# Own PSUM tiles for the experts' first products, expert operands on one base modulo 256 bytes, and a new priority table

## The chip, the core and the metric

The kernel runs on one core of a Trainium2 chip. The metric is device time in microseconds (us) of one execution; three runs of the kernel before are shown with their median. Five engines work side by side, each on its own instruction queue: PE (TensorE, matmuls), DVE (VectorE), ACT (ScalarE), POOL (GpSimd) and SP (which only issues DMAs here). An instruction waits at the head of its queue until what it needs is there; what stands behind it on that engine waits with it.

## The reference

Attention with 4 sink keys and a window of 128 keys (batch 4, 8 heads, 768 positions, head size 64), then a mixture of 8 experts with the two best experts per token (3072 tokens, 512 features, 1024 hidden):

```python
scores = np.where(is_sink | in_window, scale * q @ k.T, -1e9)
a = softmax(scores); x = (a @ v) as [3072, 512]
noisy = x @ w_gate + log1p(exp(x @ w_noise)) * noise
top2 = the two largest of noisy per token, their weights a softmax over the two
for e in range(8):
    h = np.maximum(x[rows of e] @ w1[e], 0.0)
    out[rows of e] += weight * (h @ w2[e])
```

## The kernel before, in words

Every piece of work is recorded as an operation with an engine, a modelled duration and a priority (`Plan.op`); `Plan.run` then simulates the engines and emits the instructions of each engine in the order that this list schedule gives. The priorities of the attention and routing operations come out of one table of numbers, `PR`. There are two plans, emitted one behind the other: `phase_one` (attention, routing of the first three batches, the first rows and weights of expert 0) and `phase_two` (routing of the last batch, all experts).

Attention runs over 48 steps (16 pairs of heads, 3 blocks of 256 queries): scores on PE (L315, into the PSUM tile `S`), softmax on DVE, ACT and POOL (`mn`, `cbuf`, `sm`), transposes of the weights (L380) and of the sink part (L397, from `pcbuf`), products with the values (L406, L409, L418), rows out. Each batch ends with its logits (L601, transposed back by L609) and its routing: ranks by matmul (L714 to L720), the place of each token in its expert's list (L806, `idg`). With the places known, an indirect DMA gathers rows (L891, later L897), DVE scales them (L942), they are transposed (PE, L952, for expert 0; DVE, L957, for the others) and split into a high part `skn` (ACT, L966) and a rest `sqn` (DVE, L215).

Each expert's rows are cut into two pieces of at most 512 rows. For each piece, the hidden features go in 8 blocks of 128. A block has an "up" (`up_block`): 12 matmuls of the piece's width, L1048 to L1050, that sum w1 times rows into one PSUM half `H`; then ACT writes the relu's high part (`up_h`, L1097), DVE the rest (`up_l`, L1105), both into `h`; and later a "down" (`down`, L1116 to L1118, L1121 and L1122 for the last tile) multiplies `h` with w2 (two tiles, `w2a` and `w2b`) into the PSUM banks `Y`. PE runs the up of a block while the rests of an earlier block are made, then the downs of that earlier block. In the last piece all eight ups come first and then all downs (`apart`). The finished rows are scaled (L1125) and added to the output by an indirect DMA (L1140).

`H` and `X` (PSUM for transposes and routing of the second phase) are not tiles of their own: they are the two halves of one `S` tile each, handed out by `plan.views`:

```python
pair = plan.get("S", room(sh) + 1, [128, 2, 512], F32, "wide")
plan.views["X"] = lambda i: pair[:, i % 2]
plan.views["H"] = lambda i: plan.get("S", room(sh))[:, i % 2]
```

Waits between engines are set per tile. Thus the relu of a block (ACT) also waits for the rest of the block before it (DVE), because both halves count as one tile: of the 128 relu instructions L1097, 90 carry a wait on DVE. `up_ahead` records the first two ups of expert 0 (24 matmuls) already in `phase_one`, so they stand between the last logits.

Of the kernel before, what the change touches and what calls it, by code (L numbers as in the profile page):

```python
# [20 lines left out]
PR = dict(cur=-8431.651, cur1=-7439.283, cur1_0=218.223, cur1_9=-1416.941, cur_0=0.0, cur_9=-191.213, dv=-2620.133,  # L21
          dv_0=-188.761, dv_9=-58.0, exps=-79.031, exps_0=-733.766, exps_9=-686.771, ga=0.0, gt=185.39, lg=-1781.795,
          load_qk=4173.715, load_v=245.644, mins=-994.502, mins_0=35.968, mins_9=5432.878, nosink=-4343.446,
          nosink_0=462.054, nosink_9=43.061, pcopy=-1854.216, pcopy_0=972.034, pcopy_9=77.513, plow=-3587.377,
          plow_0=-204.859, plow_9=-701.943, prev=-1305.7, prev_0=-151.842, prev_9=314.934, ptr=-349.555,
          ptr_0=-1749.435, ptr_9=-10.037, ptr_c=-3954.256, ptr_c_0=-264.44, ptr_c_9=56.179, ptr_m=-1635.596,
          ptr_m_0=182.224, ptr_m_9=-0.973, pv=-632.746, pv_0=479.582, pv_9=-76.04, pv_c=-4613.603, pv_c_0=-4.393,
          pv_c_9=16.777, qk=-1178.393, qk_0=631.58, qk_9=-3710.152, rows_c=12808.825, rows_c_0=-665.082,
          rows_c_9=-7472.954, rt=-15225.06, sink_c=-3756.417, sink_c_0=0.0, sink_c_9=16.368, sinks=-2.103,
          sinks_0=1336.99, sinks_9=-790.624, sub=-299.026, sub_0=1233.464, sub_9=50.854, sums=0.0, sums_0=723.554,  # L30
          sums_9=-13.305, sums_i=-3243.012, sums_i_0=-939.503, sums_i_9=-291.364, w1=4288.053, pctr_0=777.383,
          pctr=0.0, pctr_9=57.978, ga_l=-998.334, gt_l=111.981, ll=0.0, ua=22395.225, dv_pool=1, sm_act=10, cm_pool=9,
          pc_pool=0, gap_8=2, et=42, gap=1, stay=2496.59)
# [3 lines left out]
COLD = 5.0  # L37
SLACK = .008
WARM = 32
FIRST = 4  # L40
AHEAD = 2
# [7 lines left out]
class Plan:  # L49
# [5 lines left out]
    def __init__(self, nc, pools, rings, cold=0.0):  # L55
        self.nc = nc
        self.pools = pools
        self.rings = dict(rings)
        self.cold = cold
        self.live = {}  # L60
        self.views = {}
        self.shapes = {}
        self.count = {}
        self.ops = []
        self.touch = {}
        self.wrote = {}

    def get(self, tag, i, shape=None, dt=F32, pool="sb", pad=None):
        kx = (tag, i)
        if tag in self.views:  # L70
            x = self.views[tag](i)
            if shape is None:
                shape = self.shapes[kx]
            else:
                self.shapes[kx] = shape = (shape, pad)
            shape, pad = shape
            to = pad or shape
            x = x[:, :math.prod(to[1:])]
            if len(to) == 3:
                x = x.rearrange("p (a b) -> p a b", a=to[1])  # L80
            return x if to == shape else x[tuple(slice(0, n) for n in shape)]
# [163 lines left out]
def attention(tc, plan, cst, sh, kqs, v, vss, xbuf):  # L245
# [17 lines left out]

    def warm():
# [44 lines left out]
    def qk(n, a):  # L309
        g, j, _ = at(n, 2 * a)  # L310
        for h in range(2):
            r = slice(h * D, (h + 1) * D)
            p = get("S", 2 * n + a, [128, 2, 512], F32, "wide")[:, h, :2 * KW].rearrange("p (a b) -> p a b", a=2)
# [570 lines left out]
def gather(plan, nc, cst, sh, xbuf, e, t, z, after=None):  # L884
# [5 lines left out]
    def go():  # L890
        nc.gpsimd.indirect_dma_start(  # L891
            out=plan.get("xg", n, [128, sh.XW], F32, "early"), out_offset=None, in_=xbuf[:128 + (b + 1) * sh.S],
            in_offset=bass.IndirectOffsetOnAxis(ap=cst["idg"][:, t:t + 1], axis=0))

    def part(i):
        x = plan.get("xg", n, [128, sh.XW], F32, "early").rearrange("p (i d) -> p i d", d=sh.SW)
# [31 lines left out]
def rows_turn(plan, nc, cst, sh, e, t, size, ring, z):  # L928
# [15 lines left out]
    def spot():  # L944
        if ring == "S":
            return get(ring, ti, [128, 2, 512], F32, "wide")[:, 0, :].rearrange("p (c s) -> p c s", c=c)
# [92 lines left out]
def room(sh):  # L1039

    return sh.B * (sh.H // 2) * (sh.S // 128) + 1


# [7 lines left out]


def up_ahead(plan, nc, cst, sh, f, z):

    width = 128 * FIRST

    def go(i):
        up_block(plan, nc, sh, plan.get("S", room(sh), [128, 2, 512], F32, "wide")[:, f % 2, :width], 0, f, i, halves(plan, sh, 0), width)

    for i in range(sh.DM // 128):  # L1060
        plan.op("PE", 3 * (width / 2400 + .016), z, lambda i=i: go(i),
                r=[(x, 0, t) for x in ("xh", "xl") for t in range(FIRST)] + [w_tile(plan, 1, 0, f // 2)[0]], w=[("H", f)],
                u=[("S", room(sh))])


def experts(tc, plan, cst, sh, w1, w2, xbuf, out):
# [91 lines left out]
    z = 0  # L1158
# [5 lines left out]
    for q, (e, tiles, width) in enumerate(info):  # L1164
# [130 lines left out]
def phase_one(tc, nc, plan, ac, tail, cst, sh, kq, v, vs, w1, w2, xbuf, out):  # L1295
# [18 lines left out]
    def first_rows(t, ring, zg, zt):  # L1314
        gather(plan, nc, cst, sh, xbuf, 0, t, zg)
        weight(plan, nc, cst, sh, 0, t, zt)
        if ring == "S":
            plan.count["S"] = 2 * NJ * HP * sh.B - 1
# [22 lines left out]
    for f in range(AHEAD):  # L1341
# [113 lines left out]
```

## Time and profile before

| what | value |
|---|---|
| median of 3 runs | 787.09 us (786.73 to 788.6) |
| the profiled execution | 783.96 us, its span 782.3 us |
| clock of TensorE granted, mean | 0.998 of full speed |
| PE busy | 744.1 us, 95% of the span |
| DVE / ACT / POOL busy | 454.7 / 333.4 / 437.6 us |
| attention and three routings, 0 to 192 us | PE 175.6, DVE 172.0, ACT 148.8, POOL 142.5 us busy |
| experts, 270 to 500 us | PE 227.7 of 230 us busy |
| last piece's ups, 738 to 760 us | PE 16.6 of 22 us busy |

Busy time is the union of the instructions' spans on an engine. Matmuls are pipelined: one instruction's span (0.39 us for 512 columns) is longer than the step from its start to the start of the next (0.23 us), so a gap of the engine costs more than the idle time that a row shows in brackets. Until about 192 us DVE is nearly as busy as PE; from there on PE is busy all but a few per cent, and the question of each gap is what ended last before it.

### The profile page before, as it was taken

The page shows a single profiled execution, that of the slowest core. Times are in us where ns is not written, and L with a number is a line of the kernel's source. Part 1 is how long each engine was busy: PE and PEld are TensorE (multiplying, and loading weights), DVE is VectorE, ACT ScalarE, POOL GpSimd, SP SyncE. Part 2 cuts the span into 40 slices and gives each one's busy share as a digit, 9 for nine tenths or more (in the row PEclk, how much of TensorE's full clock was granted, in tenths as well). Part 3 has the DMA queues.
Part 4 walks back from the last instruction along what each step waited for, and adds up shares of the span by engine and source line. Part 5 has one row for each costly group of instructions (what it writes and reads, how often), then busy time and mean ns, then how long its engine had stood idle before and what let it go on. Part 6 is the DMA issues. An engine that isn't in the chain of part 4 may idle for free.

```text
span 782.3 us, 12963 instructions
## 1 busy us (share of the span) xinstructions
PE 744.1 (95%) x4499; PEld 618.9 (79%) x4499; DVE 454.7 (58%) x1181; ACT 333.4 (43%) x927; POOL 437.6 (56%) x625
## 2 busy tenths in 40 slices
PE   9999998789999999999999999999999999999975
PEld 4667676566778898889888987898898889888864
DVE  7889998987754554645364446526544643464210
ACT  6987996784114413341333143323413431451211
POOL 7665878875246375356727462747275473747202
PEclk9999999999999999999999999999999999999999
DMA  6568698565636753553445363517452652544213
GB/s 221 175 169 203 203 261 216 138 162 132 168 96 127 238 110 50 156 138 57 94 127 131 53 134 114 109 40 155 123 101 47 172 134 36 125 133 71 26 16 41
DMA packets 58372, 97.80 MB, mean 125 GB/s; under 512 B 19232, under 2 KB 31776, under 8 KB 58304
## 3 DMA queue, kind: packets, MB, share of 16 engines
q1 hardware_dynamic: 44928, 69.34, 30.5%
q0 software_dynamic: 13376, 27.60, 20.3%
q8 instruction: 36, 0.59, 0.3%
q14 instruction: 32, 0.26, 0.1%
HBM read 68.51 MB, written 28.40 MB: 124 GB/s over the span
## 4 chain that ended last, share of the span: by engine, by line
PE 70%; DVE 9%; issue 7%; ACT 6%; POOL 3%; DMA 3%; POOLq 0%; SPq 0%; DVEq 0%; ACTq 0%
PE S L1048 11%; PE S L1050 10%; PE S L1049 10%; PE Y L1118 9%; PE Y L1116 9%; PE Y L1117 9%; PE S L315 2%; DMA xg<-x_rows,rt_idq 2%; PE X L406 2%; ACT cbuf L346 2%; PE P L380 1%; DVE h L1105 1%; PE X L409 1%; DVE xg L942 1%; POOL out L1140 1%
## 5 line engine op out<-in xcount | busy, mean ns | idle before, releaser
L897 POOL DMA_INDIRECT xg<-x_rows,rt_idq x174 | 176.1, 1012 | 62.2 <-issue 53.3
L1105 DVE SCALAR_TENSOR_TENSOR h<-S,h 128x384 fp32r<-128x384 f32 (+4 forms) x168 | 75.7, 470 | 203.5 <-ACT h L1097 153.2
L1097 ACT ACTIVATE h<-S 128x384 fp32r<-128x384 f32 (+4 forms) x128 | 64.3, 503 | 290.8 <-PE S L1050 210.1
L1048 PE MATMUL S<-skn,w 128*128 128x384 f32 (+4 forms) x512 | 177.7, 347 | 10.0 <-DVE h L1105 10.0
L1050 PE MATMUL S<-skn,w 128*128 128x384 f32 (+4 forms) x512 | 175.9, 344 | 0.0
L1049 PE MATMUL S<-sqn,w 128*128 128x384 f32 (+4 forms) x512 | 175.6, 343 | 0.0
L1140 POOL DMA_INDIRECT out<-y,idx x53 | 91.7, 1730 | 57.5 <-ACT y L1125 40.9
L1149 POOL COPY spacer<-h 1x1 f32<-1x1 f32 x88 | 28.7, 326 | 157.6 <-ACT h L1097 156.8
L1048 PEld LDWEIGHTS S<-skn,w 128*128 128x128 f32 x512 | 96.1, 188 | 22.4 <-DVE h L1105 10.4
L1049 PEld LDWEIGHTS S<-sqn,w 128*128 128x128 f32 x512 | 96.1, 188 | 6.2
L1050 PEld LDWEIGHTS S<-skn,w 128*128 128x128 f32 x512 | 96.0, 188 | 2.5
L1118 PE MATMUL Y<-w2a,h 128*128 128x512 f32 x192 | 76.1, 397 | 2.3 <-DVE h L1105 1.8
L1116 PE MATMUL Y<-w2a,h 128*128 128x512 f32 x192 | 75.7, 394 | 0.7 <-ACT h L1097 0.7
L1116 PE MATMUL Y<-w2b,h 128*128 128x512 f32 x192 | 76.1, 396 | 0.0
L1117 PE MATMUL Y<-w2b,h 128*128 128x512 f32 x192 | 75.8, 395 | 0.0
L1118 PE MATMUL Y<-w2b,h 128*128 128x512 f32 x192 | 75.8, 395 | 0.0
L1117 PE MATMUL Y<-w2a,h 128*128 128x512 f32 x192 | 75.6, 394 | 0.0
L315 PE MATMUL S<-kq 64*128 64x264 f32 (+1 forms) x384 | 56.4, 401 | 4.3 <-DVE cbuf L325 1.6
L215 POOL TENSOR_TENSOR cbuf<-cbuf,mn 128x528 f32<-128x528 f32 x48 | 51.4, 1076 | 13.4 <-DVE mn L335 5.5
L966 ACT ACTIVATE skn<-xtn 128x512 fp32r<-128x512 f32 (+2 forms) x46 | 27.9, 606 | 61.7 <-DVE xtn L957 54.7
L346 ACT ACTIVATE cbuf<-cbuf 128x132 f32<-128x132 f32 x160 | 48.0, 314 | 6.6 <-POOL cbuf L215 6.2
L1118 PEld LDWEIGHTS Y<-w2a,h 128*128 128x128 f32 x192 | 36.1, 188 | 14.0 <-DVE h L1105 4.8
(212 smaller groups left out, 1298.3 us busy)
## 6 DMA issues: line engine op xcount, KB each, us to landing
st<-in_w1l SPq DMA_DIRECT2D x32, 512.0 KB
st<-in_w2l SPq DMA_DIRECT2D x32, 512.0 KB
kq<-in_kq SPq DMA_DIRECT2D x15, 792.0 KB
out<-zt SPq DMA_DIRECT2D x31, 256.0 KB
vn<-in_v SPq DMA_DIRECT2D x16, 384.0 KB
x_rows<-xr SPq DMA_DIRECT2D x48, 128.0 KB
xg<-x_rows,rt_idq POOLq DMA_INDIRECT x174
st<-in_vs SPq DMA_DIRECT2D x4, 256.0 KB
```

Of the source, the lines that this page charges most:

```text
L315: nc.tensor.matmul(p[:, :2 if j else 1], kq(g)[r, j // 2, 2 + j % 2, NS:], x[:, :2 if j else 1], start=True, stop=True)
L346: nc.scalar.activation(C(n)[:, u], C(n)[:, u], AF.Exp, scale=1.0 / math.sqrt(D), accum_out=get("sm", n, [128, 4])[:, u:u + 1])
L897: nc.gpsimd.indirect_dma_start(out=x[:, i, :], out_offset=None, in_=xbuf.rearrange("r (q d) -> (r q) d", d=sh.SW), in_offset=bass.Indirect ...
L1048: nc.tensor.matmul(p, w[:, 0], xh, start=(i == 0), stop=False)
L1049: nc.tensor.matmul(p, w[:, 0], xl, start=False, stop=False)
L1050: nc.tensor.matmul(p, w[:, 1], xh, start=False, stop=(i == sh.DM // 128 - 1))
L1097: nc.scalar.activation(get("h", FC * q + f, [128, 2 * 128 * FIRST], F32R)[:, :width], get("H", FC * q + f, [128, width], F32, "ps", [128, ...
L1105: nc.vector.scalar_tensor_tensor(h[:, o:o + s1 - s0], p[:, s0:s1], 0.0, h[:, s0:s1].bitcast(F32), op0=OP.max, op1=OP.subtract)
L1116: nc.tensor.matmul(p, hh, w[:, 0], start=(f == 0), stop=False)
L1117: nc.tensor.matmul(p, hh, w[:, 1], start=False, stop=False)
L1118: nc.tensor.matmul(p, hl, w[:, 0], start=False, stop=(f == FC - 1))
L1140: d = nc.gpsimd.indirect_dma_start(out=out, out_offset=bass.IndirectOffsetOnAxis(ap=c["idx"][:size(e, t), e, t:t + 1], axis=0), in_=get("y ...
```

## The change

The halves go: `H` gets two PSUM tiles of one bank each and `X` two, all four in the second phase's PSUM pool, and `S` goes back into the first phase's pool. The code for views is removed. With it goes `up_ahead`: the two first ups of expert 0 are now in the second plan like all others, behind the last logits; the relus and rests of expert 0's first piece get a priority 400 earlier. The gathered rows `xg` are padded from 2240 to 2304 bytes and a filler of 64 bytes (`even`) is put into the `tail` pool; with the order in which the tiles are made, this lays w1, w2a, w2b, `skn`, `sqn`, `h` and `xg` all to base 64 modulo 256. Before, these bases were 64 (w1), 0 (`skn`, `sqn`, w2a), 224 (w2b), 192 (`h`) and 64, 0, 192, 128, 64 (the five `xg`). The whole table `PR` is replaced; of its choices, `pc_pool` 0 to 2 moves 12 of the 48 copies into `pcbuf` from ACT to POOL. The instructions of each engine are otherwise the same in number.

```diff
-PR = dict(cur=-8431.651, cur1=-7439.283, cur1_0=218.223, cur1_9=-1416.941, cur_0=0.0, cur_9=-191.213, dv=-2620.133,
...
-          pc_pool=0, gap_8=2, et=42, gap=1, stay=2496.59)
+PR = dict(cur=-10653.273, cur1=-2090.412, cur1_0=-442.426, cur1_9=73.44, cur_0=-4.596, cur_9=0.0, dv=0.64,
...
+          ga_l=-1277.079, gt_l=1521.637, ll=320.211, ua=-4.272, sm_act=10, dv_pool=1, cm_pool=9, pc_pool=2, gap=2,
+          gap_8=3, et=36, stay=1992.355)
...
+LINE = 64
-AHEAD = 2
...
     def get(self, tag, i, shape=None, dt=F32, pool="sb", pad=None):
         kx = (tag, i)
-        if tag in self.views:
-            x = self.views[tag](i)
...
+    for i in range(2):
+        get("S", i, [128, 2, 512], F32, "ps")
...
-            out=plan.get("xg", n, [128, sh.XW], F32, "early"), out_offset=None, in_=xbuf[:128 + (b + 1) * sh.S],
+            out=plan.get("xg", n, [128, sh.XW], F32, "early", [128, LINE * -(-sh.XW // LINE)]), out_offset=None, in_=xbuf[:128 + (b + 1) * sh.S],
...
-def up_ahead(plan, nc, cst, sh, f, z):
...
-            if k >= AHEAD:
-                op("PE", UP1 * width + .19, zu, lambda q=q, f=f: up(q, f),
-                   r=[(x, e, t) for x in ("xh", "xl") for t in tiles] + [w_tile(plan, 1, e, f // 2)[0]], w=[("H", k)],
-                   u=[(nm, NP + q) for nm in ("skn", "sqn")])
-            op("ACT", .06 + width / 1200, zu, lambda q=q, f=f: up_h(q, f), r=[("H", k)], w=[("hh", k)], u=[("h", k)])
-            op("DVE", .08 + width / 950, zu, lambda q=q, f=f: up_l(q, f), r=[("H", k), ("hh", k)], w=[("hl", k)], u=[("h", k)])
+            op("PE", UP1 * width + .19, zu, lambda q=q, f=f: up(q, f),
+               r=[(x, e, t) for x in ("xh", "xl") for t in tiles] + [w_tile(plan, 1, e, f // 2)[0]], w=[("H", k)],
+               u=[(nm, NP + q) for nm in ("skn", "sqn")])
+            zh = zu if q else zu - 400
+            op("ACT", .06 + width / 1200, zh, lambda q=q, f=f: up_h(q, f), r=[("H", k)], w=[("hh", k)], u=[("h", k)])
+            op("DVE", .08 + width / 950, zh, lambda q=q, f=f: up_l(q, f), r=[("H", k), ("hh", k)], w=[("hl", k)], u=[("h", k)])
...
-    for f in range(AHEAD):
-        up_ahead(plan, nc, cst, sh, f, PR.get("ua", 60) + f)
...
-    plan.rings.update(y=4, h=9, X=2)
-    plan.count["X"] = 1
-    pair = plan.get("S", room(sh) + 1, [128, 2, 512], F32, "wide")
-    plan.views["X"] = lambda i: pair[:, i % 2]
-    plan.views["H"] = lambda i: plan.get("S", room(sh))[:, i % 2]
+    plan.rings.update(y=4, h=9, X=2, H=2, w2b=2)
+    for i in range(2):
+        plan.get("H", i, [128, 128 * FIRST], F32, "ps", [128, 512])
+    plan.get("X", 0, [128, NT + 1, sh.E], F32, "ps", [128, 64, 8])
+    plan.get("h", 0, [128, 2 * 128 * FIRST], F32R)
+    plan.get("w2b", 0, [128, 2, 1024], F32R)
...
+            tail.tile([128, 16], F32, name="even")
```

From the first down of the experts on, the instructions of every engine stand in the same order as before. What changes there is which waits they carry. On ACT, in the last piece, the relu's line is L1097 before and L1068 after; y is the scaled result. Before:

```order
L1097 ACTIVATE h<-S 128x384 [waits DVE_49,PE_49]
L1097 ACTIVATE h<-S 128x384 [waits DVE_49,PE_49,Pool_49]
L1125 ACTIVATE y<-Y,wc_77 128x512 [waits DMASW7_49,PE_49]
L1097 ACTIVATE h<-S 128x384 [waits DVE_49,Pool_49]
L1125 ACTIVATE y<-Y,wc_77 128x512 [waits DMASW1_49,PE_49,Activation_49]
L1125 ACTIVATE y<-Y,wc_77 128x512 [waits DMASW2_49,PE_49,Activation_49]
L1097 ACTIVATE h<-S 128x384 [waits PE_49,Pool_49] x4
```

And on ACT after, in the same place:

```order
L1068 ACTIVATE h<-H 128x384 [waits PE_49,Activation_49] x2
L1068 ACTIVATE h<-H 128x384 [waits PE_49,Pool_49]
L1096 ACTIVATE y<-Y,wc_77 128x512 [waits DMASW7_49,PE_49]
L1068 ACTIVATE h<-H 128x384 [waits PE_49,Pool_49]
L1096 ACTIVATE y<-Y,wc_77 128x512 [waits DMASW1_49,PE_49,Activation_49]
L1096 ACTIVATE y<-Y,wc_77 128x512 [waits DMASW2_49,PE_49,Activation_49]
L1068 ACTIVATE h<-H 128x384 [waits PE_49,Pool_49] x4
```

No row moved; the waits of the relus on DVE are gone (of the 128 relus 90 carried one, now 2). On PE, an up waits for the rest (DVE) of the block two before it, which used its bank; before, it waited for the rest of the block right before it.

On PE at the end of the first phase (L952 and L941 are the transposes of the last tile of expert 0's first rows, whose rows are gathered with the places of the third batch; X<-xtn,wbd are logits; X<-idf,lt turns them back). Before:

```order
L418 MATMUL X<-ps,vr 128x128
L609 MATMUL X<-idf,lt 128x128 x2
L1048 MATMUL S<-skn,w_1580 128x512
L1049 MATMUL S<-sqn,w_1580 128x512 [waits DVE_49]
L1050 MATMUL S<-skn,w_1580 128x512
L601 MATMUL X<-xtn,wbd 32x256 [waits Activation_49]
L601 MATMUL X<-xtn,wbd 32x256 x3
L609 MATMUL X<-idf,lt 128x128 [waits Activation_49]
L609 MATMUL X<-idf,lt 128x128
L1048 MATMUL S<-skn,w_1580 128x512
```

And on PE after:

```order
L590 MATMUL X<-xtn,wbd 32x256 [waits Activation_49]
L941 MATMUL S<-idf,xg 128x128 [waits DMASW3_49,DVE_49]
L941 MATMUL S<-idf,xg 128x128 x3
L598 MATMUL X<-idf,lt 128x128 [waits Activation_49]
L598 MATMUL X<-idf,lt 128x128
L598 MATMUL X<-idf,lt 128x128 [waits Activation_49]
L598 MATMUL X<-idf,lt 128x128
L1032 MATMUL H<-skn,w_1607 128x512 [waits DVE_49,PE_49]
L1033 MATMUL H<-sqn,w_1607 128x512
```

The transposes of the last tile stood ahead of the last two attention steps' products with the values (L406); they moved to right behind the last logits. The first up stood between the logits; it now stands behind all of them and behind those transposes. The placing of the third batch (L806, now L795) moved too: six of the 48 products with the values stood behind it before, three stand behind it now.

## Rows read from the trace of the kernel before

**Rows 1.** The page, part 1: busy us, share of the span, instructions of each engine

```profile
PE 744.1 (95%) x4499; PEld 618.9 (79%) x4499; DVE 454.7 (58%) x1181; ACT 333.4 (43%) x927; POOL 437.6 (56%) x625
```

**Rows 2.** Busy in the first stretch: PE, PEld, DVE, ACT, POOL, clock, DMA, GB/s

```profile
0.00:192.00 192.00, 175.60 (x1694) 121.20 (x1694) 172.01 (x507) 148.84 (x636) 142.45 (x247) 1.00 0.68 188
```

**Rows 3.** Waits of PE, whole run: us in total, times, longest us

```profile
PE S L1048 <- DVE h L1105: 10.0, 10, 1.6
...
PE Y L1118 <- DVE h L1105: 1.8, 6, 0.5
```

**Rows 4.** The same view, from 240 us on (its L1048 row is unchanged)

```profile
PE Y L1118 <- DVE h L1105: 1.3, 5, 0.3
PE Y L1118 <- DVE gw L1031: 0.5, 2, 0.3
```

**Rows 5.** Timeline of PE, last piece: start, duration, [idle before <- what ended it]

```profile
743.08 0.34 PE L1050 MATMUL S<-skn,w 128*128 128x384 f32 x1
744.64 0.44 PE L1048 MATMUL S<-skn,w 128*128 128x384 f32 x1 [1.23 <-DVE h L1105]
744.92 0.34 PE L1049 MATMUL S<-sqn,w 128*128 128x384 f32 x1
...
746.67 0.34 PE L1050 MATMUL S<-skn,w 128*128 128x384 f32 x1
```

**Rows 6.** Timeline of ACT and DVE in the same place

```profile
743.51 0.49 ACT L1097 ACTIVATE h<-S 128x384 fp32r<-128x384 f32 x1 [4.02 <-PE S L1050]
...
744.03 0.56 DVE L1105 SCALAR_TENSOR_TENSOR h<-S,h 128x384 fp32r<-128x384 f32 x1 [5.11 <-ACT h L1097]
```

**Rows 7.** Timeline of DVE and PE around 350 us

```profile
350.15 0.56 DVE L1105 SCALAR_TENSOR_TENSOR h<-S,h 128x384 fp32r<-128x384 f32 x1 [1.99 <-PE S L1050]
...
350.77 0.50 PE L1118 MATMUL Y<-w2a,h 128*128 128x512 f32 x1 [0.26 <-DVE h L1105]
351.10 0.39 PE L1116 MATMUL Y<-w2a,h 128*128 128x512 f32 x1
```

**Rows 8.** Timeline of DVE around 260 us, behind a gather

```profile
260.34 0.16 DVE L1031 TENSOR_TENSOR gw<-xg,perm 32x8 f32<-32x8 f32 x1 [2.93 <-DMA xg<-x_rows,rt_idq]
...
261.97 0.52 DVE L1105 SCALAR_TENSOR_TENSOR h<-S,h 128x256 fp32r<-128x256 f32 x2
```

**Rows 9.** Timeline of PE: first and last of 9, then of 11 downs

```profile
301.93 0.40 PE L1116 MATMUL Y<-w2b,h 128*128 128x512 f32 x1
...
303.80 0.39 PE L1118 MATMUL Y<-w2b,h 128*128 128x512 f32 x1
...
306.45 0.39 PE L1116 MATMUL Y<-w2a,h 128*128 128x512 f32 x1
...
308.74 0.39 PE L1118 MATMUL Y<-w2a,h 128*128 128x512 f32 x1
```

**Rows 10.** Timeline of PE around 165 us: operands on unequal, then on equal bases

```profile
165.04 0.66 PE L380 MATMUL P<-idf,cbuf 128*128 128x128 f32 x4
165.46 0.64 PE L418 MATMUL X<-ps,vr 128*128 128x128 f32 x4
```

**Rows 11.** Timeline of PE, POOL and DVE: from the placing to the first downs

```profile
168.40 0.54 PE L806 MATMUL X<-rt_tc,rt_op 128*128 128x56 f16 x12
...
171.76 1.09 POOL L891 DMA_INDIRECT xg<-x_rows,idg  x1 [0.17 <-issue]
172.87 0.26 POOL L215 TENSOR_TENSOR pcbuf<-cbuf,pcbuf 128x32 fp32r<-128x32 f32 x1
...
177.93 0.90 DVE L942 TENSOR_TENSOR xg<-xg 128x512 f32<-128x512 f32 x1
...
182.30 0.68 DVE L215 TENSOR_TENSOR sqn<-S,skn 128x512 fp32r<-128x512 f32 x1
...
188.19 0.38 PE L609 MATMUL X<-idf,lt 128*128 128x128 f32 x2
...
194.08 0.50 PE L1118 MATMUL Y<-w2a,h 128*128 128x512 f32 x1 [0.55 <-DVE h L1105]
```

More of the change, by code (lines that the diff above doesn't have):

```diff
@@ L69, in get @@
         kx = (tag, i)
-        if tag in self.views:
-            x = self.views[tag](i)
[L72 to L81, printed above, removed]
         if kx not in self.live:
@@ L312, in qk @@
             r = slice(h * D, (h + 1) * D)
-            p = get("S", 2 * n + a, [128, 2, 512], F32, "wide")[:, h, :2 * KW].rearrange("p (a b) -> p a b", a=2)
+            p = get("S", 2 * n + a, [128, 2, 512], F32, "ps")[:, h, :2 * KW].rearrange("p (a b) -> p a b", a=2)
             x = keys(g, max(j - 1, 0))[r]
@@ L891, in go @@
         nc.gpsimd.indirect_dma_start(
-            out=plan.get("xg", n, [128, sh.XW], F32, "early"), out_offset=None, in_=xbuf[:128 + (b + 1) * sh.S],
+            out=plan.get("xg", n, [128, sh.XW], F32, "early", [128, LINE * -(-sh.XW // LINE)]), out_offset=None, in_=xbuf[:128 + (b + 1) * sh.S],
             in_offset=bass.IndirectOffsetOnAxis(ap=cst["idg"][:, t:t + 1], axis=0))
     def part(i):
-        x = plan.get("xg", n, [128, sh.XW], F32, "early").rearrange("p (i d) -> p i d", d=sh.SW)
+        x = plan.get("xg", n, [128, sh.XW], F32, "early", [128, LINE * -(-sh.XW // LINE)]).rearrange("p (i d) -> p i d", d=sh.SW)
         nc.gpsimd.indirect_dma_start(
@@ L945, in spot @@
         if ring == "S":
-            return get(ring, ti, [128, 2, 512], F32, "wide")[:, 0, :].rearrange("p (c s) -> p c s", c=c)
+            return get(ring, ti, [128, 2, 512], F32, "ps")[:, 0, :].rearrange("p (c s) -> p c s", c=c)
         return get(ring, ti, [128, c, 128], F32, "ps")
@@ L1050, in up_block @@
     nc.tensor.matmul(p, w[:, 1], xh, start=False, stop=(i == sh.DM // 128 - 1))
-def up_ahead(plan, nc, cst, sh, f, z):
[L1055 to L1063, printed above, removed]
 def experts(tc, plan, cst, sh, w1, w2, xbuf, out):
@@ L1317, in first_rows @@
         if ring == "S":
-            plan.count["S"] = 2 * NJ * HP * sh.B - 1
+            plan.count["S"] = 2 * NJ * HP * sh.B
         rows_turn(plan, nc, cst, sh, 0, t, 128, ring, zt)
@@ L1382, in moe_kernel @@
         experts_setup(nc, cst, sh, consts)
-        wide = both.enter_context(tc.tile_pool(name="wide", bufs=1, space=bass.MemoryType.PSUM))
-        pools = {"tail": tail, "early": early, "wide": wide}
+        pools = {"tail": tail, "early": early}
         with ExitStack() as st:
+            tail.tile([128, 16], F32, name="even")
             ac = st.enter_context(tc.tile_pool(name="ac", bufs=1))
@@ L1394, in moe_kernel @@
             plan.run()
-            live = {kx: t for kx, t in plan.live.items() if kx[0] in ("st", "w1", "w2a", "xtn", "ri", "xg", "skn", "sqn", "lg", "S")}
+            live = {kx: t for kx, t in plan.live.items() if kx[0] in ("st", "w1", "w2a", "xtn", "ri", "xg", "skn", "sqn", "lg")}
         sb = both.enter_context(tc.tile_pool(name="msb", bufs=1, reuse_waits="tile"))
         ps = both.enter_context(tc.tile_pool(name="mps", bufs=1, space=bass.MemoryType.PSUM, reuse_waits="tile"))
-        p2 = Plan(nc, {"sb": sb, "ps": ps, **pools}, {kx: plan.rings[kx] for kx in ("st", "xtn", "ri", "xg", "lg", "S")})
+        p2 = Plan(nc, {"sb": sb, "ps": ps, **pools}, {kx: plan.rings[kx] for kx in ("st", "xtn", "ri", "xg", "lg")})
         p2.live.update(live)
```

25 lines of the change are left out of this document (10 added, 15 removed).

## The prediction

> **What bounds the kernel now.** I read the page's busy times first: PE is busy 95% of the span [rows 1], so only what PE itself does or waits for can move the end. The stretches come next: up to 192 us DVE is busy 172.0 us, PE 175.6 and ACT and POOL 149 and 142 [rows 2], so there the four engines wait for each other in turn and the order decides; from there on PE has nearly no idle time left but its waits. The view of PE's waits names them: 10.0 us in 10 waits of the up (L1048) for DVE's rest of a block, and small ones of the down (L1118) [rows 3]. All ten of the ups' waits lie behind 240 us, and of the downs' waits 1.3 and 0.5 us in 7 [rows 4].
>
> Why an up has to wait is seen in the last piece. An up ends at 743.08 + 0.34 = 743.42, ACT's relu runs from 743.51, DVE's rest from 744.03 to 744.59, and only then does the next up start, at 744.64 [rows 5, 6]. The next up writes the other half of the tile, which nobody reads; it waits because both halves are one tile. The same rule has two more faces. Around 350 us DVE leaves a rest standing until 350.15, released by PE's L1050 of the next up, and the down that needs the rest comes late, at 350.77 [rows 7]. Around 260 us DVE stands 2.93 us until 260.34 behind a gather, with the rest of a block queued behind it until 261.97 [rows 8], and the next up waits for that rest.
>
> **The change, part by part.**
>
> *Own tiles for H.* What a wait costs PE is more than its idle time. The idle time counts from the modelled end of the last matmul (0.34 us after its start), but the next could have started one step after it: the step is (746.67 - 744.92)/10 = 0.175 us [rows 5], so 0.165 us come on top, and the first matmul behind the wait takes 0.28 us to the next instead of 0.175 [rows 5]. That is 0.27 us for each wait; for a down (0.33 us from 350.77 to 351.10 against a step of 0.23 [rows 7, 9]) it comes out the same. The sum from 240 us on: idle 10.0 + 1.3 + 0.5 = 11.8, plus 17 waits x 0.27 = 4.6, together 16.4 us.
>
> With own tiles an up waits only for the rest two blocks back. In the last piece an up of 12 x 0.175 = 2.1 us covers the chain from an up's end to its rest's end (743.42 to 744.59, 1.17 us), so that wait falls to nothing with 0.9 us to spare. Around 350 us the relu and the rest wait for their own up alone, and the rest is through before its down. Behind a gather the next up no longer waits for the queued rest; it runs while DVE catches up. Such an up has 12 steps of about 0.148 us (320 columns: the 0.175 of 384 less 64 columns at 2.4 a ns), 1.8 us, and the longest of the waits was 1.6 [rows 3], so the rest is there when the down behind the up wants it. This cover holds by 0.2 us; if it does not, the waits behind gathers, some 4 us of the 16.4, shrink to the gather's lateness instead of going. I take the whole 16.4 and keep 12 as the lower end.
>
> *The first two ups behind the logits.* They used to fill PE between the last logits: the first of their 24 matmuls ran at 185.07, the last logit transpose at 188.19, and the second down's last part started at 194.08 [rows 11], itself after two waits for the shared tile. Now 24 ups of 0.233 us (a 512 wide step with w2b is (303.80 - 301.93)/8 = 0.234, with w2a (308.74 - 306.45)/10 = 0.229 [rows 9]) and two downs follow the last logits: 5.6 + 0.5 = 6.1 us. If the logits end as before, that point comes at 194.4, 0.3 us later. But the ups also need the last tile's rows, and these hang on the placing of the third batch: from 168.40 over the gather's issue at 171.76, the scaling at 177.93 to the rest at 182.30 + 0.68 it took 14.6 us [rows 11]. The placing now has three steps of attention behind it, not six. If a half of the 19.8 us from 168.40 to 188.19 remains behind it, it comes at about 178.3, the rows are ready at 192.9, and the point moves to 199.0: 4.9 us later. In that case PE stands idle in front of the last tile's transposes or of the first up, and everything behind it waits. The chain was stretched by busy engines (the gather's issue came 3.4 us after the placing), and the new order puts less beside it, so I take +2 us, between the ends of 0 and +5.
>
> *The new order of the first phase.* The same instructions run in another order; 12 copies of about 0.26 us [rows 11] go from ACT to POOL, 3.1 us, and both have over 40 us free in this stretch [rows 2]. The trace of before shows no order but its own. DVE needs 172 us and PE 175.6 of the 192, so the order leaves at most 16 us to gain and has no such floor for a loss. I take 0, with 4 us to either side, a quarter of that slack.
>
> *Own tiles for X.* They take one wait of about a microsecond away at the transposes of the second rows; their operands hang on a gather, so I count nothing.
>
> *Bases modulo 256.* Downs with w2a (base 0, `h` 192) step at 229 ns and with w2b (224, `h` 192) at 234 [rows 9]. If all w2b downs went at w2a's step, 616 x 4 ns give -2.4 us; if all w2a downs went at w2b's, +2.4. The only matmuls of before with equal bases (L418, both at 96) take 0.64 us for four, those with unequal ones (L380) 0.66 [rows 10], so equal bases as such cost nothing to be seen at 128 columns. I take -1 and keep -2.5 to +2.5.
> The Trainium skill's "SBUF — State Buffer" (Who interferes with whom) lists two independent read ports for PE, one for the moving operand and one for weights, and says that PE never waits on anyone. By that rule the bases would do nothing, and the -1 would be 0; the rows on four matmuls agree, the difference of 5 ns between w2a and w2b is not explained by it.
>
> *Sum.* 782.3 - 16.4 + 2 + 0 - 1 = 766.9 us of span. The profiled execution took 783.96, 1.66 more than its span; that gives 768.6. The median of the runs, 787.09, lies 3.1 above the profiled execution, so the forecast is **771.7**, told as 772. With the ends of each term (4.4 less gain, transition 0 to 5, order 4 up or down, bases 2.5) taken in part together, its own range is 764 to 779.
>
> **The rivals.**
>
> *The end of the first phase takes most of it.* The waits go, but the last tile's rows come late as in the upper end above (+5) and the new order loses 4 more: 772 + 3 + 4 + 1 (no gain of the bases) = 780. For it: the first up now hangs on a gather that is placed later. Against: DVE and POOL had work of other steps between the links of that chain.
>
> *The waits were not the shared tile's.* If the relu and rest come late for another reason (the gathers, DVE's own queue), the tiles change nothing, and the new order is left: 787 with -4 to +6. Against: in the last piece ACT and DVE stand idle 4 and 5 us before the relu and the rest [rows 6] and nothing else is queued.
>
> *Slower: equal bases make PE's two reads meet.* Every one of some 2,770 matmuls of the experts would pay. From 16.4 - 2 + 2.4 (a change that can be told) = 17 us on, about 6 ns each, it decides; at a step of 236 to 240 for 229 to 234, 7 ns each, it costs 19.4 us: 772 + 1 + 19.4 = 792. For it: no row of before has long matmuls with equal bases. Against: [rows 10].
>
> *The bases were what holds the step up.* A step of 229 to 234 at 512 columns lies 16 to 21 ns above 512/2.4 = 213 ns, at the granted clock of 1.00; 0.175 at 384 lies 15 above 160. If most of this, 12 ns, came from unlike bases, 2,770 x 12 = 33 us would go: 772 + 1 - 33 = 740. Against: unlike pairs of bases (w1 64 with rows at 0, w2a 0 with `h` 192) all show about the same excess.
> The Trainium skill's "TensorE: Matmul & The Clock Gate" (Back-to-back issue gap) puts the step of a warm matmul at N/2.4 plus about 2.5 ns; the trace does not agree, it has 16 to 21. By that figure the excess to be gained would be about 14 ns, or 39 us, and the time an estimated 734.
>
> **How the numbers follow.** Chances: forecast 0.74; first phase takes most of it 0.11; waits not the tile's 0.04; slower by equal bases 0.06; bases give much 0.05. A difference of 0.3%, 2.4 us, is about what a measurement of this kernel can tell from none. Faster (under 784.7): 0.74 + 0.11 + 0.05, less a small part of the second case, 0.89. Within: 0.04. Slower (over 789.4): 0.07, the slower rival and an order that loses more than the tiles give. The range reaches from 762 to 781: the forecast's own and the first rival.
>
> **What would show it.** The view of PE's waits from 240 us on has no L1048 row over 1 us, and the relu (now L1068) waits for PE's last up matmul and no longer for DVE; the last eight ups run without a gap. At the first up a wait for DVE's `sqn` or, ahead of it, of L941 for the gather tells how much of the +2 to +5 is there, and the start of the second down's last part (194.08) tells it in sum. The steps of nine downs with w2b tell the bases: 234 ns stays, 229 or less gains, over 236 loses. The prediction is wrong if the waits go and reappear as waits of the down for the rest, or if the experts' first down comes more than 8 us later.

## The result, and the profile after

| | before | after |
|---|---|---|
| median of 4 runs each, taken together | 787.38 us (786.73 to 788.6) | 773.51 us (773.13 to 774.06) |
| ratio, with its 95% interval | | 0.9823 (0.9806 to 0.984) |
| the profiled execution, and its span | 783.96, 782.3 us | 773.13, 771.4 us |
| the mark: first L1118 (L1089 after) starts | 194.08 us | 202.12 us |
| from there to the end of the span | 588.2 us | 569.3 us |

The mark is the last part of the experts' first down; the prediction and the expectations call it the second down's last part.

The changed kernel is 1.8% faster, 773.51 us where 772 was forecast, inside the range and on the expected side. The two last lines show that two things of opposite sign happened: the experts became 18.9 us shorter, and they begin 8.0 us later.

The page's part 1 after (busy us, share of the span, instructions), to be held against [rows 1]:

```profile
PE 740.0 (96%) x4499; PEld 624.2 (81%) x4499; DVE 458.3 (59%) x1181; ACT 334.3 (43%) x915; POOL 439.7 (57%) x637
```

PE has the same 4499 instructions; twelve went from ACT to POOL (915 for 927, 637 for 625). The view of PE's waits from 200 us on, after (us in total, times, longest us), has a single row:

```profile
PE X L941 <- DVE xg L931: 0.7, 1, 0.7
```

The ten waits of [rows 3] and the seven of [rows 4] are gone. Why is seen in the last piece, on ACT and then on DVE (start, duration, what ended the idle time before it), to be held against [rows 6]:

```profile
738.84 0.49 ACT L1068 ACTIVATE h<-H 128x384 fp32r<-128x384 f32 x1 [1.59 <-PE H L1034]
...
740.92 0.49 ACT L1068 ACTIVATE h<-H 128x384 fp32r<-128x384 f32 x1 [1.59 <-PE H L1034]
```

```profile
739.37 0.56 DVE L1076 SCALAR_TENSOR_TENSOR h<-H,h 128x384 fp32r<-128x384 f32 x1 [1.52 <-ACT h L1068]
```

Two relus stand 2.08 us apart, which is one up: 12 matmuls of 0.173 us. Before, the up, the relu and the rest ran one after the other. Now the rest of a block (until 739.93) runs beside the next up, which goes on: in the last of the windows below PE is busy for all 20 us.

The windows of after around the end of the first phase and in the experts (PE, PEld, DVE, ACT, POOL, clock, DMA, GB/s):

```profile
182.00:187.00 5.00, 0.63 (x4) 0.29 (x3) 3.04 (x10) 0.00 (x0) 1.69 (x3) 0.61 0.12 19
187.00:193.00 6.00, 5.45 (x41) 4.37 (x44) 3.20 (x6) 1.12 (x4) 4.18 (x6) 0.50 0.52 160
```

```profile
500.00:730.00 230.00, 230.00 (x1148) 207.44 (x1147) 114.41 (x254) 75.43 (x119) 128.09 (x162) 1.00 0.42 99
730.00:750.00 20.00, 20.00 (x110) 19.05 (x109) 4.46 (x8) 6.01 (x11) 4.86 (x6) 1.00 0.31 41
```

From 500 to 750 us PE is busy throughout. The loss is in one place: from 182 to 187 us PE works for 0.63 us of 5, ACT not at all, and the six microseconds behind it run at a granted clock of 0.50, which is the 1.2 GHz level. What PE does there (timeline of PE, after):

```profile
178.09 0.47 PE L795 MATMUL X<-rt_tc,rt_op 128*128 128x56 f16 x12
...
186.72 0.47 PE L386 MATMUL X<-idf,pcbuf 128*128 128x128 f32 x1 [4.37 <-POOL pcbuf L201]
187.13 1.12 PE L395 MATMUL X<-CT,vn 128*64 128x128 f32 x8
...
202.12 0.39 PE L1089 MATMUL Y<-w2a,h 128*128 128x512 f32 x1
```

PE does not wait for the gather or for its rows. It waits for a small add into `pcbuf` on POOL (L201), which one of the last attention steps needs. POOL and SP show what holds that add (timelines of POOL, then of SP's DMA issues, after):

```profile
185.30 1.09 POOL L880 DMA_INDIRECT xg<-x_rows,idg  x1 [5.70 <-DMA out<-zt]
186.40 0.28 POOL L201 TENSOR_TENSOR pcbuf<-cbuf,pcbuf 128x32 fp32r<-128x32 f32 x1
```

```profile
169.97 6.93 SPq L426 DMA_DIRECT2D x_rows<-xr  x12
177.00 2.45 SPq L729 DMA_DIRECT2D x_rows<-rt_w  x4
179.49 0.54 SPq L1262 DMA_DIRECT2D out<-zt  x1
```

The gather of the last tile's rows reads what these writes put into memory: 12 writes of attention rows and 4 of routing weights (`rt_w`) for the third batch. SP issues them one behind another, the last until 179.45. The places (`idg`) are made by DVE at 179.86; the gather starts only at 185.30, after 5.70 us in which POOL does nothing. The profile puts the wait down to the zeroing write issued right behind them; the `rt_w` writes, which the gather needs, stand just ahead, 5.9 us before the gather starts. (The experiment with two queues shows below that it is `rt_w`.) In the kernel before, `rt_w` was issued from 163.01 on and the gather started at 171.76 [rows 11], with other work on POOL between. Its issues on SP, and the piece of the chain view that leads to that gather (start, duration):

```profile
163.01 3.24 SPq L740 DMA_DIRECT2D x_rows<-rt_w  x4
```

```profile
164.62 5.70 DMA x_rows<-rt_w
```

So this write landed only at 170.32, 1.4 us ahead of the gather: the chain was there before the change, with little to spare. After, POOL has the weights ready at 171.55 (163.30 before), and they then stand until 177.00 behind the twelve row writes in SP's queue.

Behind the waiting gather stands the `pcbuf` add, behind that add PE, and behind PE's pause the lower clock: the eight L395 matmuls that took 0.66 us at full clock take 1.12.

### The profile page after: what moved, and what is told of

Same layout as the page of the kernel before. It is cut to its first block, busy times and chain, and to the rows that moved or that the text cites. A ratio compares the mean times of both kernels' runs of the same rounds, so it can differ in the third digit from the quotient of the medians.

```text
span 771.4 us, 12927 instructions
## 1 busy us (share of the span) xinstructions
PE 740.0 (96%) x4499; PEld 624.2 (81%) x4499; DVE 458.3 (59%) x1181; ACT 334.3 (43%) x915; POOL 439.7 (57%) x637
## 4 chain that ended last, share of the span: by engine, by line
PE 64%; issue 4%; DMA 3%; POOL 2%; DVE 1%; ACT 0%; SPq 0%; POOLq 0%; ACTq 0%
PE H L1034 11%; PE H L1033 11%; PE H L1032 11%; PE Y L1088 10%; PE Y L1089 10%; PE Y L1087 10%; POOL out L1111 1%; PE Y L1092 1%; PE Y L1093 1%; DMA out<-y,idx 1%; DMA xg<-x_rows,idg 1%; DMA st<-in_w1l 1%; DMA out<-zt 1%; SPq L1262 0%; PE X L941 0%
## 5 line engine op out<-in xcount | busy, mean ns | idle before, releaser
L1068 ACT ACTIVATE h<-H 128x384 fp32r<-128x384 f32 (+4 forms) x128 | 64.6, 505 | 268.5 <-PE H L1034 235.8
L1076 DVE SCALAR_TENSOR_TENSOR h<-H,h 128x384 fp32r<-128x384 f32 (+4 forms) x168 | 75.8, 471 | 173.4 <-ACT h L1068 159.0
L1034 PE MATMUL H<-skn,w 128*128 128x384 f32 (+4 forms) x512 | 175.9, 344 | 0.0
L1032 PE MATMUL H<-skn,w 128*128 128x384 f32 (+4 forms) x512 | 175.7, 343 | 0.1
L1033 PE MATMUL H<-sqn,w 128*128 128x384 f32 (+4 forms) x512 | 175.6, 343 | 0.1
L1111 POOL DMA_INDIRECT out<-y,idx x53 | 93.8, 1770 | 49.8 <-ACT y L1096 33.5
L1032 PEld LDWEIGHTS H<-skn,w 128*128 128x128 f32 x512 | 96.2, 188 | 7.3 <-PE X L598 0.3
L1033 PEld LDWEIGHTS H<-sqn,w 128*128 128x128 f32 x512 | 96.1, 188 | 7.2 <-DVE sqn L201 0.5
L1034 PEld LDWEIGHTS H<-skn,w 128*128 128x128 f32 x512 | 96.0, 188 | 2.2
L1089 PE MATMUL Y<-w2a,h 128*128 128x512 f32 x192 | 75.6, 394 | 0.0
L1089 PE MATMUL Y<-w2b,h 128*128 128x512 f32 x192 | 75.5, 393 | 0.0
L201 POOL TENSOR_TENSOR cbuf<-cbuf,mn 128x528 f32<-128x528 f32 x48 | 53.0, 1104 | 22.4 <-DVE mn L324 9.7
L304 PEld LDWEIGHTS S<-kq 64*128 64x128 f32 x384 | 30.6, 189 | 21.0 <-DVE cbuf L314 9.9
```

The source lines that it names most:

```text
L201: eng.tensor_tensor(out, a, b, op=OP.subtract)
L304: nc.tensor.matmul(p[:, :2 if j else 1], kq(g)[r, j // 2, 2 + j % 2, NS:], x[:, :2 if j else 1], start=True, stop=True)
L1032: nc.tensor.matmul(p, w[:, 0], xh, start=(i == 0), stop=False)
L1033: nc.tensor.matmul(p, w[:, 0], xl, start=False, stop=False)
L1034: nc.tensor.matmul(p, w[:, 1], xh, start=False, stop=(i == sh.DM // 128 - 1))
L1068: nc.scalar.activation(get("h", FC * q + f, [128, 2 * 128 * FIRST], F32R)[:, :width], get("H", FC * q + f, [128, width], F32, "ps", [128, ...
```

## The experiments

The theory put to the test: own tiles for H bring all of the experts' gain; the new table loses at the end of the first phase because writes, and not the placing, release the gather; the bases bring about 2 us, because a matmul's two operands lie on the same base modulo 256. The rivals: the waits were not the shared tile's; the loss comes from the two ups put behind the logits; the absolute base counts, or the bases do nothing.

All ratios are to the kernel before in the same rounds; its medians there were 785.6 to 786.5 us.

**The changed kernel again.** No edit.

> The changed kernel as it is, on the chip and in the rounds of the other runs of this set, as the mark for small differences. Theory and rival alike: 0.982 to 0.984 of the kernel before; second down's last part at about 202, a wait of PE of over 4 us at 182 to 187 behind the last gather.

774.53 us, ratio 0.9844 (0.982 to 0.9868), span 773.7 us. Gather at 186.53 behind 6.24 us of idle POOL, PE's wait for `pcbuf` 4.90 us, the mark at 204.59. The stall is no accident of one execution; its place moves by 2.5 us between two of them, and with it the span.

**H as the halves of one tile again.** All else as changed.

```diff
-    for i in range(2):
-        plan.get("H", i, [128, 128 * FIRST], F32, "ps", [128, 512])
+    halves_h = plan.pools["ps"].tile([128, 2, 512], F32, name="H")
+    plan.views["H"] = lambda i: halves_h[:, i % 2]
```

> The changed kernel with one edit: H is again the two halves of one PSUM tile; X, bases, order and table stay as changed. Theory: the waits of the relus for the rest of the block before come back with about 16.5 us of PE time from 240 us on, all of it in waits of the up and the down for DVE's rest; the end of the first phase stays late (second down's last part at about 202). Time 790, against 773.5 of the changed kernel. Rival (the gain came from something else, bases or the order): 773 to 776, and no such waits of over 1 us.

793.25 us, ratio 1.0091 (1.0061 to 1.0122): without the own tiles, the rest of the change is slower than the kernel before. Waits of PE in this run from 205 us on (us, times, longest; the rest is L1090 here, the up L1046, the down L1103):

```profile
PE H L1046 <- DVE h L1090: 9.8, 10, 1.3
PE Y L1103 <- DVE h L1090: 1.3, 5, 0.3
...
PE Y L1103 <- DVE gw L1034: 0.5, 2, 0.3
```

They are [rows 3] and [rows 4] again, 17 waits. From the mark (204.91) to the end of the span (791.3) it is 586.4 us, with own tiles 569.3 (569.1 in the second execution). **17.1 us** is what the tiles bring there; the sum by idle time plus 0.27 us for each wait had said 16.4. (The medians differ by 18.7 to 19.7 us; the mark is late here too, and the first downs ahead of it wait as they did before.) That the waits were not the shared tile's is thereby ruled out.

**X as the halves of one tile again.** The same edit for X.

> The changed kernel with X as the two halves of one PSUM tile again; H keeps its own tiles, bases, order and table stay as changed. Theory: one wait of about a microsecond at the transposes of the second rows comes back, 0 to 1.5 us slower than the changed kernel, 774 to 776. Rival (X's tiles carry a part of the gain in the experts): 4 us or more slower, with waits of PE from 205 us on.

774.5 us, ratio 0.985 (0.9814 to 0.9887). The wait is back (PE's waits):

```profile
PE X L955 <- DVE rt_idq L860: 1.7, 1, 1.7
```

and the time is that of the changed kernel. The 1.7 us is within what its executions differ by; nothing can be said beyond that.

**The table of before.** The changed kernel with the old `PR`.

```diff
-PR = dict(cur=-10653.273, cur1=-2090.412, ...
-          gap_8=3, et=36, stay=1992.355)
+PR = dict(cur=-8431.651, cur1=-7439.283, ...
+          pc_pool=0, gap_8=2, et=42, gap=1, stay=2496.59)
```

> The changed kernel with the table PR of the kernel before; own tiles and bases stay as changed, the first two ups stay behind the logits. Theory: in the new order the third batch's rows are turned on DVE and written late, which held up the last gather; with the old table the writes come as in the kernel before and the second down's last part comes at 195 to 198 instead of 202: 767 to 769. Rival (the 8 us come from the ups that no longer fill the gaps between the logits, whatever the table): 773 to 774.

**764.06 us** (763.53 to 765.72), ratio 0.9715 (0.9682 to 0.9748): faster than both kernels. PE, POOL and SP's issues in this run, and its window:

```profile
170.51 0.51 PE L795 MATMUL X<-rt_tc,rt_op 128*128 128x56 f16 x12
...
195.40 0.39 PE L1089 MATMUL Y<-w2a,h 128*128 128x512 f32 x1
```

```profile
173.84 1.09 POOL L880 DMA_INDIRECT xg<-x_rows,idg  x1 [0.17 <-issue]
```

```profile
165.09 2.20 SPq L729 DMA_DIRECT2D x_rows<-rt_w  x4
```

```profile
182.00:189.00 7.00, 6.42 (x74) 3.94 (x72) 6.85 (x19) 4.55 (x12) 4.18 (x8) 1.00 0.39 105
```

The routing weights are issued 12 us earlier, the gather waits for nothing but its turn, the clock stays at 1.00 there, and the mark comes at 195.40 for 202.12, 6.7 us earlier.

That is less than the table costs. Up to 183 us PE runs the same matmuls in the same order here as in the kernel before, and there the placing started at 168.40 [rows 11]; here it starts at 170.51, 2.1 us later. The delay comes from far ahead (windows, the kernel before and then this run):

```profile
54.00:57.00 3.00, 3.00 (x42) 2.26 (x36) 1.67 (x5) 2.76 (x16) 1.74 (x4) 1.00 0.92 199
```

```profile
54.00:57.00 3.00, 3.00 (x24) 1.40 (x24) 1.40 (x4) 2.08 (x11) 1.70 (x4) 0.50 0.70 163
```

In this execution the clock was at the 1.2 GHz level from 54 to 57 us, after PE had been busy for 2.3 of four microseconds; in the kernel before it stayed at 1.00, and no run tells why. Without that stretch the mark would lie at about 193.3, so the new table costs about **8.8 us** at this point, an estimate from 6.7 and 2.1. The spans agree: 763.5 us in this execution and 761.4 and 761.5 in the two with a mean clock of 0.998, for 771.4 as changed.

**The ups behind the logits alone.** The table of before, H and X as halves, the old bases except `w2b`'s (96 for 224): what is left is the place of the first two ups, with the earlier priority of expert 0's first relus and rests that goes with it.

> The kernel before with one part of the change alone: the first two ups of expert 0 no longer stand between the last logits, but behind them in the second plan. Table, shared halves of H and of X and the bases stay those of the kernel before (w2b lies on 96 instead of 224). Theory (prediction's step: 0.3 to 5 us lost there, +2 taken; the run with the old table had its second down's last part 1.3 us late with own tiles, which save two waits there): 2 to 4 us slower than the kernel before, 788 to 790 against 786. Rival (the missing filler is what cost the changed kernel its 8 us): 794.

788.67 us, ratio 1.0033 (1.0017 to 1.0048). The placing, the mark, and the same window as above:

```profile
170.32 0.52 PE L809 MATMUL X<-rt_tc,rt_op 128*128 128x56 f16 x12
...
196.51 0.51 PE L1103 MATMUL Y<-w2a,h 128*128 128x512 f32 x1
```

```profile
54.00:57.00 3.00, 3.00 (x28) 1.40 (x27) 1.31 (x3) 2.09 (x11) 1.69 (x4) 0.54 0.79 170
```

The mark comes at 196.51 for 194.08, 2.4 us later, but 1.9 us of that are there already at the placing (170.32 for 168.40), from the same stretch at 1.2 GHz; the ups come behind it. From the placing to the mark it is 26.2 us for 25.7: the two ups cost **0.5 us**, near the 0.3 that the prediction gave for logits that end as before. The run with the old table takes 24.9 us for the same way, so the unshared tiles take 1.3 us off at the first downs. The rival, 794, is refuted. The median is 2.2 us above that of the kernel before, and not all of it is the ups' doing: 1.5 us of the span lie behind the mark (589.7 for 588.2), where `w2b` lies on another base.

**Row turns of the third batch earlier.** With the new table, DVE turns the third batch's rows (L421) as soon as they are there; SP can then write them early.

```diff
-            op("DVE", .285, n + .7 + P(g, "rows_c"), lambda n=n: rows(n), ...
+            op("DVE", .285, n + .7 + (P(g, "rows_c") if b != sh.B - 2 else 0), lambda n=n: rows(n), ...
```

> The changed kernel with one edit: the row turns (DVE) of the third batch get the priority of their own step, without the table's offset of about 10,000, so that their writes to memory no longer start behind the logits of that batch. Theory: the last gather then waits only for its places (about 180 us) and no longer until 185.3; PE's wait of 4.4 us behind it and the stretch at half clock go: 766 to 769. Rival (the writes are not what the gather waited for): the gather still starts at about 185 and the time stays at 773.

779.12 us, ratio 0.9922 (0.9896 to 0.9948): slower than as changed, where a gain was expected. The expected time was wrong; that the gather waited for writes holds. PE and POOL in this run:

```profile
174.53 0.18 PE L703 MATMUL X<-m,tri 128*128 128x48 bf16 x1 [1.70 <-DVE sqn L201]
...
185.86 0.47 PE L795 MATMUL X<-rt_tc,rt_op 128*128 128x56 f16 x12
```

```profile
186.88 1.09 POOL L880 DMA_INDIRECT xg<-x_rows,idg  x1 [0.86 <-DVE ids L862]
```

The row writes now lie at 144 to 155 us and the gather follows the placing by 1.0 us, where it was 7.2: the wait for the writes is gone. But the placing itself went from 178.09 to 185.86. Two causes are in sight, and no run tells them apart: the turns take DVE's time, and the rank matmuls (L703) start behind DVE at 174.53, as changed at 170.2; and the granted clock of this execution was 0.50 from 128.5 to 135 and again from 176.5 to 183 us, both ahead of the placing. This one number, moved alone, did not mend it; the old table had writes and placing early.

**Half of those writes through ACT's queue.** Eight of the sixteen writes of the third batch issued by ACT.

```diff
-            nc.sync.dma_start(dram(xbuf, (128 + b * S + jj * 256) * XW ...
+            (nc.scalar if b == sh.B - 2 and q % 2 else nc.sync).dma_start(dram(xbuf, (128 + b * S + jj * 256) * XW ...
```

(and the same in the writes of `rt_w`)

> The changed kernel with one edit: of the third batch's writes of rows and routing weights, 8 of 16 are issued by ACT's queue instead of SP's; the order of all computing instructions is unchanged. Theory (the last gather waits for these writes, which SP issues one after the other in 9.4 us from 170 on): the issues end at about 175 instead of 179.5, the gather starts at 180 to 182 instead of 185.3, PE's wait behind it falls from 4.4 us to about 1 or less, and the time by 3 to 5 us against the changed kernel. Rival (the gather's wait is for the landing of the many small packets, or for another transfer): the gather still starts at about 185 and the time stays.

773.39 us, ratio 0.9837 (0.9807 to 0.9866), as without the edit. ACT's issues, and the gather:

```profile
178.03 1.65 ACTq L729 DMA_DIRECT2D x_rows<-rt_w  x2
```

```profile
185.64 1.08 POOL L880 DMA_INDIRECT xg<-x_rows,idg  x1 [4.39 <-DVE lg L606]
```

ACT was late itself, its last issue ended at 179.68 (SP's alone 179.45), and the gather again came 6.0 us behind it. So the run does not tell what an earlier issue would have brought. But it tells which DMA the gather waits for, because here the zeroing write was issued at 177.03, ahead of ACT's two `rt_w` writes, and landed at 182.9. POOL's four waits for DMAs, just ahead of the gather, end later:

```profile
L880 POOLq EVENT_SEMAPHORE  x4: 43/43/43, 184.2 to 184.8; - x4
```

ACT's `rt_w` writes, issued at 178.03 and 178.88, landed 6.2 and 5.8 us later, at 184.2 and 184.7. The gather waits for these. The profile itself names now the one DMA and now the other; the landing times decide it. The chain view of the second execution of the changed kernel names the same write, from its issue to 1.1 us ahead of the gather:

```profile
179.54 5.91 DMA x_rows<-rt_w
```

**The old bases.** The changed kernel without the padding of `xg`, the filler and the order in which the tiles are made.

> The changed kernel with the padding of xg, the filler and the early creation of h and w2b taken out: the bases modulo 256 are those of the kernel before (w1 64, skn and sqn 0, w2a 0, w2b 224, h 192, xg 64, 0, 192, 128, 64), the instructions and their order are unchanged. Theory, from the steps in the two traces (about 2,750 matmuls, 0.7 ns each): 2 us slower, 775.5, with w2b's steps back at 233 to 234 ns and w2a's at 229 to 230. Rival 1 (the bases do nothing, the difference of the traces has another cause): 773.5, steps as in the changed kernel. Rival 2 (unlike bases are better): 771.

776.44 us, ratio 0.9879 (0.9845 to 0.9913); as changed 0.9823 and 0.9844. The interval lies just above that of the first of these and overlaps that of the second, so the runs alone don't settle it; the steps do. First and last of twelve downs with `w2b` (11 steps), and then the last matmuls of the first and of the second up (12 steps), after:

```profile
760.55 0.39 PE L1087 MATMUL Y<-w2b,h 128*128 128x512 f32 x1
...
763.04 0.39 PE L1089 MATMUL Y<-w2b,h 128*128 128x512 f32 x1
```

```profile
198.72 0.39 PE L1034 MATMUL H<-skn,w 128*128 128x512 f32 x1
...
201.44 0.39 PE L1034 MATMUL H<-skn,w 128*128 128x512 f32 x1
```

and the same with the old bases:

```profile
761.20 0.40 PE L1087 MATMUL Y<-w2b,h 128*128 128x512 f32 x1
...
763.75 0.39 PE L1089 MATMUL Y<-w2b,h 128*128 128x512 f32 x1
```

```profile
198.64 0.40 PE L1034 MATMUL H<-skn,w 128*128 128x512 f32 x1
...
201.44 0.39 PE L1034 MATMUL H<-skn,w 128*128 128x512 f32 x1
```

2.49/11 = 226 ns for 2.55/11 = 232, and 2.72/12 = 227 for 2.80/12 = 233. Over the whole run, the mean step with `w2b` is 16.6 ns above 512/2.4 = 213.3 as changed and 19.4 with the old bases, that of the 512 wide ups 13.8 and 19.7, while `w2a` (16.6 and 16.7) and the 384 wide ups (15.3 and 14.8) hardly move. Summed over 2,760 steps the excess is 43.2 us for 45.1: the bases bring **1.9 us**.

**All operands on base 224, and on base 0.** A filler of 160 and of 192 bytes among the constants shifts all of them together.

```diff
+    pool.tile([128, 40], F32, name="shift")
```

(48 instead of 40 for base 0)

> The changed kernel with a filler of 160 bytes ahead of all tiles: the experts' operands stay on one common base modulo 256, but that is 224 instead of 64. Theory A (what counts is that the two operands of a matmul have the same base): steps as in the changed kernel, 16.6 ns over 512/2.4 for the downs, 13.8 for the 512 wide ups; same time. Theory B (what counts is where the moving operand itself starts, 224 being no multiple of 64): the downs with w2a and w2b both at about 19.5 ns, 1,220 x 2.9 = 3.5 us slower, and the ups up too.

> As the run with base 224, with a filler of 192 bytes: all on base 0 modulo 256. Theory A (same base counts): steps as in the changed kernel, the 512 wide ups at 13.8 ns over 512/2.4. Theory B (the start of the moving operand counts): the 512 wide ups at about 19.7 as in the kernel before, whose rows lay on 0, the downs with w2a and w2b at 16.7 as w2a's in the kernel before.

774.72 us, ratio 0.9856 (0.9826 to 0.9886), on base 224, and 772.35 us in a single execution on base 0. Twelve downs with `w2b` on base 224, and ten ups' last parts (9 steps) on base 0:

```profile
762.03 0.39 PE L1088 MATMUL Y<-w2b,h 128*128 128x512 f32 x1
...
764.53 0.39 PE L1090 MATMUL Y<-w2b,h 128*128 128x512 f32 x1
```

```profile
203.53 0.39 PE L1033 MATMUL H<-skn,w 128*128 128x512 f32 x1
...
205.57 0.39 PE L1033 MATMUL H<-skn,w 128*128 128x512 f32 x1
```

2.50/11 and 2.04/9 are both 227 ns, as on base 64; the excess summed is 43.2 us again on either base. So it does not count where the operands lie, as long as both lie alike. That unlike bases always cost something is not shown: `w2a`, with operands 64 bytes apart, steps as fast as with equal ones.

## Why the prediction was right, and which steps were not

- **Own tiles for H: right, in mechanism and size.** 17.1 us for 16.4. The part that counted 0.27 us beyond the idle time for each of 17 waits was needed: idle time alone, 11.8 us, would have been 5.3 short. The cover behind the gathers (1.8 us of up for 1.6 us of wait) held; no wait of a down for the rest appeared in its place.
- **The first two ups: right in sign, too large.** +0.5 us for +2, seen apart with the old table. The prediction's own first case, logits that end as before, gave 0.3; the +2 was taken because the late placing was counted in this term too.
- **The new order of the first phase: this is the step that failed.** It was put at 0 with ends of 4 us to either side, "a quarter of that slack"; it cost about 8.8 us. The ends were taken from how much the engines had free over 192 us, and the loss came from one chain. The prediction had seen that the placing would come later, and its 178.3 us was met within 0.2 (178.09). But it followed the chain from the placing to the gather alone, and took the gather's other operand, the rows and weights in memory, as there. In the kernel before they were, by 1.4 us: the landing of `rt_w` stands in its chain view right ahead of the gather. The new table puts twelve row turns and sixteen writes through DVE and SP's queue until 179.45, and so the gather starts 5.3 us after its places are known. From the placing to the first up it took 18 us (178.09 to 196.14), where 14.6 was carried over as what the old order took, to fall if anything. The prediction also looked for PE's pause in front of the last tile's transposes or of the first up; it came two attention steps earlier, at an add that stood behind the gather on POOL. Asking for each step that is moved which queues it is moved past would have found both: SP's issues and POOL's order were there to be read.
- **The place of the mark** moved by 8.0 us, where 0 to 5 was given, for this reason. The prediction's own sign of being wrong, the first down more than 8 us later, came true: 201.67 for 192.80, 8.9 us.
- **Bases: right in sign, small.** -1.9 us for -1, inside the ends of -2.5 and +2.5. The rival that equal bases make two reads meet is refuted, since the steps became shorter in sum; so is the one that unlike bases make up most of the excess, since 16.6 and 13.8 ns of it are left when all are equal.
- **X: nothing to be seen**, as counted.
- **The offset.** The median of before lay 3.1 us above its profiled execution, and the same was added after; there it was 0.4 us (773.51 for 773.13). This made the forecast 2.7 us too long. The profiled execution of the kernel before, at a mean granted clock of 0.998, was one of its shortest, so the 3.1 was no constant to carry over.

Added up in spans: -17.1 (H) + 0.5 (the ups) - 1.3 (the unshared tiles at the first downs) + 8.8 (the table) - 1.9 (bases) = -11.0 us; measured 771.4 - 782.3 = -10.9. The forecast's span was 766.9, 4.5 us too short: the table's 8.8 us were missed, and the other terms together brought 4.4 us more than was forecast. Its offset was 2.7 us too long. That the 772 came within 1.8 us is luck, because these misses have opposite signs; that the experts' gain was right is not. Without the new table the same change gives 764.06 us.

What stays open: which of the table's numbers moves the turns and writes. Of them only the row turns of one batch were tried alone, and there the placing came late. `rt_w` is late for two reasons, the routing on POOL (8 us) and the row writes ahead of it on SP (5.5 us), and no run takes one of them away without moving something else.

## What to carry to other kernels

Two buffers that take turns need a tile each where waits are set per tile: as halves of one tile the relu, the rest and the next product run in a row, which cost 17.1 of 782 us here, more than the idle time of the waits shows. A new order is priced by what each gather or DMA needs in memory and through which queue that gets there, not by how busy the engines are on the mean; one late write at the head of a chain stopped POOL and PE, and PE's clock fell. Before a difference at one mark is put down to an edit, a mark ahead of the edit is compared too: here 1.9 of 2.4 us had come from a stretch at the lower clock more than 100 us earlier. And a table tuned together with a change should also be run apart from it: the old table with the new tiles was the best version of all, 764.06 us.

## What the runs showed of the hardware

- The step of a matmul can depend on where its two operands lie in relation to each other. Excess over the columns' time at a granted clock of 1.00: 512 wide ups, bases 64 apart, 19.7 ns, equal 13.8; downs 32 apart (`w2b` 224, `h` 192) 19.4, 96 apart (the kernel with the ups moved alone) 20.2, equal 16.6; downs 64 apart (`w2a` 0, `h` 192) 16.7, equal 16.6; 384 wide ups 64 apart 14.8, equal 15.3, so that equal bases are the slower ones there. Why 64 bytes matter for the 512 wide ups and not for `w2a` was not found, and no run tells whether 256 is the right modulus.
  The Trainium skill's "SBUF — State Buffer" (Who interferes with whom) says that PE never waits on anyone. That is said of other engines; the steps here, longer by 3 to 6 ns with nothing changed but the addresses of PE's own operands, are outside of what it covers.
- Of 43 us of excess over the columns' time in 2,760 steps, none went with the choice of the common base: it was there on each of the bases 0, 64 and 224. Unlike bases added 1.9. No run says what the rest is.
- While PE waited for 4.4 us (from 182.35 on), the granted clock fell to the 1.2 GHz level; it was 0.61 from 182 to 187 and 0.50 from 187 to 193 us, and the eight small products L395 took 1.12 us for 0.66. With the old table, which has no such pause there, it was 1.00 from 182 to 189.
- The clock can differ between executions of one order of matmuls: at 54 to 57 us it was 1.00 in the kernel before, and 0.50 and 0.54 in the two runs with the old table's order, which were 1.9 to 2.1 us late from there on.
- Four `rt_w` writes of 36 KB each, in small pieces, had their gather 5.9 to 6.4 us behind the end of the last issue in four runs where nothing else held that gather (as changed twice, two queues, H as halves); in the three whose profile has the landing, it came 5.8 to 5.9 us after the start of that issue.
